# Token tiles 2 to 15 of the normalised input, transposed by DMA instead of by TensorE and ScalarE

## The chip, the core and the metric

The kernel runs on one core of one Trainium2 chip. A core has a matrix engine (TensorE, "PE" in the profile), a vector engine (VectorE, "DVE"), an activation engine (ScalarE, "ACT"), a general engine (GpSimd, "POOL") and a queue engine that starts DMA transfers (SyncE, "SP"). Each runs its own list of instructions in order, and they wait for each other by semaphores. The metric is the device time of one execution in microseconds.

## The reference, cut to what matters

One sequence of 2048 tokens with 1024 features goes through a layer norm. Its result `xn` feeds two branches: attention with 32 heads of 32 features, and a second layer norm with an MLP of 3584 hidden features. All is bf16 in and out.

```python
x = A_x                                  # 2048 x 1024
xn = _layernorm(x)
qkv = xn @ wqkv                          # q, k, v: 32 heads of 32
p = softmax(q @ k.T * 32 ** -0.5)
s = (p @ v) @ wo
y = _layernorm(xn)
h = gelu(y @ w1 + b1)                    # 3584 hidden
g = silu(h @ w2 + b2)
return x + s * g
```

Every product contracts over features, and TensorE contracts over partitions. So `xn`, which is computed with tokens on the partitions, is needed with features on the partitions. That is the transpose this case is about.

## The kernel before, in words

**An order made ahead of time.** The kernel is written as a list of operations, each with what it reads and writes, a guessed duration and a priority. The class `_Plan` runs them through a small model of the engines when the program is built (`run`), and so fixes the order of each engine's instructions. `settle` then works out the fewest semaphore waits, and `emit` (line 524 is where an instruction is put out) writes the program. The guessed durations and priorities decide the order. They do not decide when an instruction runs on the chip: there, an engine takes the next instruction of its list, waits for its semaphores and runs it. A queue is as strict for SP: a DMA that waits holds up all DMAs behind it.

**Tiles and pairs.** The 2048 tokens are 16 tiles of 128 (`NT`), and 8 pairs of tiles (`NPR`).

**The prologue** works on tiles in order:

- `load_x` (line 719): SP loads a tile of `x`, 128 x 1024 bf16, into `xst`. The tiles lie in memory that later holds the hidden activations `hT` (tiles 0 to 9) and the second-layer weights `w2r` (tiles 10 to 15), so the profile shows them under these names.
- DVE takes mean and variance: two `bn_stats` (line 860) and a `bn_aggr` (line 862) a tile, then two small operations per pair (lines 875 and 877).
- POOL takes the power -1/2 for a pair (line 879), a product (line 881), and normalises each tile (line 889) into one of four buffers `xnb[t % 4]`. Three of them lie in `gw` and the fourth in `yT`, and so the profile names them. Tiles 0 and 1 are normalised by DVE (line 870).
- `tr_item`: TensorE transposes the eight 128 x 128 blocks of a tile with an identity matrix into PSUM (line 840), and ACT copies them to `xnT`, "big" in the profile (line 851). For half of tile 1 the copy is DVE's (line 849).
- `k_pair_item`: TensorE makes the keys of head group 0 for a pair of tiles (8 matmuls, `ps<-big,qk`), and DVE casts them (line 805). `v_item` does the same for the values of a pair (16 matmuls, `ps<-qk,big`, cast in line 777), two pairs behind (`VLAG`).
- At the end of the prologue POOL computes the factors of the second layer norm for all tiles (lines 899 to 903). The last of these is a power over 128 x 16 numbers. DVE makes two diagonal matrices from it (line 944), with which `make_y` scales `xnT` for the MLP.

**Attention** runs in units. A unit is four heads, 256 queries and 256 keys. For a unit TensorE makes scores (line 1116), ACT two exponentials of 128 x 1024 (line 1125). VectorE adds up the weights of several units (lines 1146, 1151, 1154), and TensorE multiplies the weights by the values and by ones (line 700). Units run in order. The first eight, 0 to 7, use the keys of pairs 0 to 7 with the queries of pair 0, so that unit k can start once the keys of pair k are there. Between the units TensorE does the MLP products, the projections of the next heads and, at the end, the output products (line 705), spread by the planner.

**SP** also loads the weights: `load_qk` (line 730), `load_v` (line 735), `load_w1` (line 927) and `load_w2` (line 933), with priority 3.

Of the kernel before, what the change touches and what calls it, by code (L numbers as in the profile page):

```python
# [39 lines left out]
DN = ()  # L40
EVD = ()
PART = 5
ENGS = ("PE", "ACT", "DVE", "POOL", "SP")


# [18 lines left out]
class _Plan:  # L64
# [48 lines left out]
    def run(self, total_units, dense_slack):  # L113
# [7 lines left out]
        state = {"mode": "c", "bw": 0.0, "s": 0, "pv": 0, "pvopen": None, "dopen": None, "susp": None,  # L121
                 "done": 0.0, "last_bank": 7}
# [19 lines left out]
        def commit(o, t):  # L142
            e = o.eng
            o.start = t
            if e == "SP":
                if o.prio >= 5:
                    for x in reversed(order["PE"]):
                        if x.fin <= t:
                            o.deps[x] = True
                            break  # L150
                tf[e] = t + o.occ
                state["bw"] = max(state["bw"], t) + o.nbytes / 280.0
                o.fin = state["bw"] + 1900.0
            else:
                tf[e] = t + o.occ
                o.fin = t + o.occ + o.lat
            order[e].append(o)
            self.seq.append(o)
            release(o, t)
            wake(tf[e], e)  # L160
# [265 lines left out]
        while ev:  # L426
            t, ei = heapq.heappop(ev)
            e = ENGS[ei]
# [8 lines left out]
            o = pick(e, t)  # L437
# [97 lines left out]
def bass_recurrent_scan__mha_block__mixer_channel_mlp__prompt_kernel(  # L535
# [16 lines left out]
    NT = S // 128  # L552
# [12 lines left out]
    x2 = A_x.rearrange("b s d -> (b s) d")  # L565
# [6 lines left out]
    add = plan.add  # L572

    with ExitStack() as st:
# [14 lines left out]
        xnT = big[:].rearrange("p (c s) -> p c s", c=DC)  # L589
# [4 lines left out]
        wqk = [qk0[:, 4096 + i * 1024:4096 + (i + 1) * 1024].rearrange("p (c n) -> p c n", c=DC) for i in range(3)]  # L594
# [11 lines left out]
        w1r = [sb(f"w1r{i}", [128, DC, 256], BF16) for i in range(NW1R)]  # L606
# [21 lines left out]
        lnp = sb("lnp", [128, NT, 6], F32)  # L628
# [5 lines left out]
        xst = [h_flat[:, i * 1024:(i + 1) * 1024] for i in range(10)] + \  # L634
# [52 lines left out]
        def pool(fn, occ, R, W, prio=3):  # L687
            return add("POOL", fn, occ, PL, R, W, prio)

        def dma(sem, fn, nbytes, R, W, prio=3, extra=()):  # L690
            return add("SP", fn, 430, 0, R, W, prio, sem=sem, nbytes=nbytes, extra=extra)
# [18 lines left out]
        XS = lambda i: ("xst", i)  # L710
# [3 lines left out]
        for i in range(10, 16):  # L714
            lo, hi = (i - 10) * 1024, (i - 9) * 1024
            al_x[i] = [("w2", k) for k in range(NW2R) if k * 1792 < hi and (k + 1) * 1792 > lo]

        def load_x(t):
            dma(f"x{t}", lambda e: e.dma_start(xst[t], x2[t * 128:(t + 1) * 128, :]), 262144, [], [XS(t)] + al_x_w(t))

        def al_x_w(t):
            return []

        nqk = {"n": 0}

        def load_qk(hg, which):
            i = nqk["n"] % 3
            nqk["n"] += 1
            src = A_wqkv[:, which * D + hg * 128: which * D + (hg + 1) * 128].rearrange("(c p) n -> p c n", p=128)
            dma(f"wqk{i}", lambda e: e.dma_start(wqk[i], src), 262144 * 3 // 2, [], [("wqk", i)])  # L730
            return i

        def load_v(pr):
# [7 lines left out]
        for t in range(XF, 6):  # L741
            load_x(t)
        load_v(0)
        for t in range(6, NT):
            load_x(t)
        pool(lambda e: e.iota(iota_i, pattern=[[1, 128]], base=0, channel_multiplier=-1), 300, [], [("iota",)])
        dve(lambda e: e.tensor_single_scalar(ident[:], iota_i, 0, op=ALU.is_equal), 220, [("iota",)], [("ident",)], 0)
# [33 lines left out]
        def k_pair_item(n, with_q):  # L781
            return pair_item(n, (1, 0) if with_q else (1,))
# [69 lines left out]
            return it  # L852

        pro_q = plan.queues["pro"]
        XV = lambda t: ("xst", t)
        pro_q.append(warm_item())
        for n in range(NPR):
            for t in (2 * n, 2 * n + 1):
                for c in range(2):
                    dve(lambda e, t=t, c=c: e.bn_stats(stats[:, t, c, :], xst[t][:, c * 512:(c + 1) * 512]),  # L860
                        600, [XS(t)], [("st", t, c)], 1)
                dve(lambda e, t=t: e.bn_aggr(mv[:, t, :], stats[:, t, :, :].rearrange("p c s -> p (c s)")),
                    150, [("st", t, 0), ("st", t, 1)], [("mv", t)], 1)
            lo, hi = 2 * n, 2 * n + 2
            if n == 0:
                for t in (0, 1):
# [16 lines left out]
            for t in (lo, lo + 1):  # L883
                if t in DN:
                    dve(lambda e, t=t: e.tensor_scalar(xnb[t % 4], xst[t], mv[:, t, 0:1], lnp[:, t, 1:2],
                                                       op0=ALU.subtract, op1=ALU.mult), 75 + 0.26 * 1024,
                        [XS(t), ("mv", t), ("rs", n)], [("xnb", t % 4)], 0.5)
                    continue
                pool(lambda e, t=t: e.tensor_scalar(xnb[t % 4], xst[t], lnp[:, t, 1:2], lnp[:, t, 5:6],  # L889
                                                    op0=ALU.mult, op1=ALU.add), 950,  # L890
                     [XS(t), ("nb_", n), ("rs", n)], [("xnb", t % 4)], 1)
            pro_q += [tr_item(lo), tr_item(lo + 1), k_pair_item(n, False)]
            if n >= VLAG:
                pro_q.append(v_item(0, n - VLAG, "pro"))
        pro_q.append(q_pair_item(1))
# [27 lines left out]
        def load_w1(p):  # L923
            gi = p % NW1R
            pi = p % NW1
            src = B_w1[:, pi * 256:(pi + 1) * 256].rearrange("(c p) f -> p c f", p=128)
            dma(f"w1{gi}", lambda e: e.dma_start(w1r[gi][:], src), 524288, [], [("w1", gi)])

        def load_w2(q, r):
            i = nw2["n"] % NW2R  # L930
# [475 lines left out]
```

## Time and profile before

| | us |
|---|---|
| median of 3 runs | 1066.99 |
| the three runs | 1066.93 to 1067.59 |
| the profiled execution | 1066.99 |
| its span, from the first instruction to the last | 1064.9 |
| granted TensorE clock, mean | 0.996 |

The first 47 us hold the prologue. Some of the groups of the profile in that window:

| operation | line, engine | count | mean us |
|---|---|---|---|
| transposes of a block, `ps<-ident,gw` and `ps<-ident,yT` | 840, PE | 96 + 32 | 0.24 and 0.22 |
| eviction of a tile's transposes, 128 x 1024 | 851, ACT | 15 | 1.03 |
| exponential, 128 x 1024 | 1125, ACT | 15 | 1.03 |
| normalisation of a tile | 889, POOL | 14 | 1.19 to 1.41 |
| power for a pair | 879, POOL | 7 | 0.85 |

Matmuls are pipelined: eight transposes of a tile take 0.62 us together, not eight times their mean.

The DMA transfers of the first 60 us, with the median time from issue to landing: an input tile of 256 KB 4.4 us (tiles 0 to 9) and 6.7 us (tiles 10 to 15), a first-layer weight block of 512 KB 9.5 us, a second-layer weight block of 448 KB 3.7 us, the bias b2 (256 KB) 3.6 us.

How to read it: busy shares are averages over the whole span, so the share of an engine in one stage is taken from a table of windows. A timeline line gives start, length, engine, line, operation and tiles. Numbers in square brackets are the idle time of the engine before, and what ended it.

### The profile page before, as it was taken

The page shows a single profiled execution, that of the slowest core. Times are in us where ns is not written, and L with a number is a line of the kernel's source. Part 1 is how long each engine was busy: PE and PEld are TensorE (multiplying, and loading weights), DVE is VectorE, ACT ScalarE, POOL GpSimd, SP SyncE. Part 2 cuts the span into 40 slices and gives each one's busy share as a digit, 9 for nine tenths or more (in the row PEclk, how much of TensorE's full clock was granted, in tenths as well). Part 3 has the DMA queues.
Part 4 walks back from the last instruction along what each step waited for, and adds up shares of the span by engine and source line. Part 5 has one row for each costly group of instructions (what it writes and reads, how often), then busy time and mean ns, then how long its engine had stood idle before and what let it go on. Part 6 is the DMA issues. An engine that isn't in the chain of part 4 may idle for free.

```text
span 1064.9 us, 32134 instructions
## 1 busy us (share of the span) xinstructions
PE 1024.6 (96%) x14338; PEld 637.8 (60%) x14338; DVE 977.4 (92%) x1513; ACT 1024.3 (96%) x1114; POOL 34.0 (3%) x42
## 2 busy tenths in 40 slices
PE   7898999999999999999999999999999999999997
PEld 5655466646666556656666566656666566664442
DVE  8899999998899999898899999999999899978897
ACT  4899999999999999999999999999999999999993
POOL 5600000000000000000000000000000000000000
PEclk9999999999999999999999999999999999999999
DMA  9334257723276446723375446533475577772431
GB/s 267 90 105 130 59 163 202 208 82 86 79 213 184 113 113 194 200 75 105 103 201 159 142 130 188 166 90 88 134 210 166 166 236 205 220 208 89 148 110 50
DMA packets 285795, 156.48 MB, mean 147 GB/s; under 512 B 23642, under 2 KB 276570, under 8 KB 285658
## 3 DMA queue, kind: packets, MB, share of 16 engines
q1 hardware_dynamic: 285658, 154.44, 50.9%
q8 instruction: 112, 1.84, 0.7%
q14 instruction: 25, 0.20, 0.1%
HBM read 142.35 MB, written 12.06 MB: 145 GB/s over the span
## 4 chain that ended last, share of the span: by engine, by line
ACT 46%; PE 45%; DVE 4%; DMA 3%; POOL 1%; issue 0%; DVEq 0%; POOLq 0%
ACT P L1125 43%; PE ps L705 30%; PE ps L1116 8%; PE ps L700 7%; DMA w1r<-in_B_w_dram 3%; ACT ut L991 3%; DVE ut L860 1%; DVE PA L1146 0%; ACT gw L1027 0%; POOL gw L889 0%; POOL lnp L903 0%; DMA hT<-in_A_x_dram 0%; DVE xb L976 0%; DVE V L777 0%; DVE PA L1151 0%
## 5 line engine op out<-in xcount | busy, mean ns | idle before, releaser
L1125 ACT ACTIVATE P<-ps 128x1024 bf16<-128x1024 f32 x1024 | 960.9, 1198 | 10.8 <-PE ps L1116 10.5
L1146 DVE TENSOR_TENSOR PA<-P 128x2048 bf16<-128x2048 bf16 x251 | 303.9, 1212 | 17.1 <-ACT P L1125 15.9
L705 PE MATMUL ps<-yT,w1r 128*128 128x256 bf16 x1792 | 232.4, 273 | 8.7 <-DMA w1r<-in_B_w_dram 6.0
L705 PE MATMUL ps<-w2r,hT 128*128 128x256 bf16 x1792 | 228.6, 274 | 1.4 <-DVE hT L994 0.6
L705 PEld LDWEIGHTS ps<-yT,w1r 128*128 128x128 bf16 x1792 | 162.4, 98 | 67.1 <-issue 32.9
L705 PEld LDWEIGHTS ps<-w2r,hT 128*128 128x128 bf16 x1792 | 162.1, 98 | 54.6 <-issue 33.6
L700 PE MATMUL ps<-P,V 128*32 128x256 bf16 x4096 | 146.0, 275 | 0.9 <-DVE V L777 0.5
L1151 DVE TENSOR_TENSOR PA<-PA 128x1024 bf16<-128x1024 bf16 x202 | 137.9, 689 | 1.7
L705 PE MATMUL ps<-big,qk 128*128 128x512 bf16 (+2 forms) x568 | 131.2, 361 | 2.6 <-DVE V L777 0.8
L705 PE MATMUL ps<-qk,big 128*128 128x256 bf16 (+1 forms) x736 | 124.9, 306 | 0.2
L700 PEld LDWEIGHTS ps<-P,V 128*32 128x32 bf16 x4096 | 97.5, 97 | 34.8 <-issue 22.8
L1116 PE MATMUL ps<-qk 32*128 32x256 bf16 x2048 | 101.9, 273 | 8.8 <-ACT P L1125 7.0
L1116 PE MATMUL ps<-QKT 32*128 32x256 bf16 x2048 | 101.7, 273 | 4.5 <-ACT P L1125 4.3
L705 PEld LDWEIGHTS ps<-qk,big 128*128 128x128 bf16 x736 | 65.4, 98 | 39.5 <-issue 15.8
L976 DVE TENSOR_TENSOR xb<-ps,b1T 128x512 bf16<-128x512 f32 x112 | 76.8, 686 | 12.0 <-PE ps L705 10.9
L705 PEld LDWEIGHTS ps<-big,qk 128*128 128x128 bf16 x568 | 48.2, 99 | 54.3 <-issue 15.0
L994 DVE SCALAR_TENSOR_TENSOR hT<-ut,xb 128x512 bf16<-128x512 f32 x112 | 74.2, 681 | 1.9 <-ACT ut L991 1.7
L1116 PEld LDWEIGHTS ps<-QKT 32*128 32x128 bf16 x2048 | 30.3, 92 | 71.9 <-ACT P L1125 67.8
L1116 PEld LDWEIGHTS ps<-qk 32*128 32x128 bf16 x2048 | 30.4, 92 | 71.7 <-ACT P L1125 62.2
L989 DVE SCALAR_TENSOR_TENSOR ut<-hT,xb 128x1024 f32<-128x1024 bf16 x56 | 68.2, 1220 | 0.1
L991 ACT ACTIVATE ut<-ut 128x1024 f32<-128x1024 f32 x56 | 67.6, 1212 | 0.0
L1200 DVE STREAM_TRANSPOSE nt<-ps 128x256 f32<-128x256 f32 x64 | 28.7, 448 | 28.2 <-PE ps L700 27.9
(79 smaller groups left out, 574.3 us busy)
## 6 DMA issues: line engine op xcount, KB each, us to landing
w1r<-in_B_w_dram SPq DMA_DIRECT2D x112, 512.0 KB, 4.5
w2r<-in_B_w_dram SPq DMA_DIRECT2D x128, 448.0 KB, 4.3
qk<-in_A_wqkv_dram SPq DMA_DIRECT2D x16, 256.0 KB, 3.7
g_scratch<-gw SPq DMA_DIRECT2D x32, 128.0 KB, 4.5
o_scratch<-ot SPq DMA_DIRECT2D x56, 64.0 KB, 3.2
big<-o_scratch SPq DMA_DIRECT2D x28, 128.0 KB, 3.9
hT<-in_A_x_dram SPq DMA_DIRECT2D x10, 256.0 KB, 4.4
qk<-in_A_wqkv_dram SPq DMA_DIRECT2D x4, 512.0 KB, 3.9
```

Of the source, the lines that this page charges most:

```text
L700: ins = e.matmul(dst(j), lhsT=lhsT(j), rhs=rhs(j), start=start, stop=stop, tile_position=(0, 32 * j), skip_group_check=True)
L705: return e.matmul(dst, lhsT=lhsT, rhs=rhs, start=start, stop=stop, skip_group_check=True)
L860: dve(lambda e, t=t, c=c: e.bn_stats(stats[:, t, c, :], xst[t][:, c * 512:(c + 1) * 512]), 600, [XS(t)], [("st", t, c)], 1)
L976: dve(lambda e: e.tensor_tensor(xb_t[i2][:, p % 2].rearrange("p (k t) -> p k t", k=2), bank(it.bank).rearrange("p (k t) -> p k t", k=2), b ...
L989: dve(lambda e, r=r: e.scalar_tensor_tensor(ut_t[i2][:, r], h[:, r], 1.0 / GA, xb[:, r], op0=ALU.add, op1=ALU.mult), c_f32(r.stop - r.star ...
L991: act(lambda e: e.activation(ut_t[i2][:], ut_t[i2][:], ACT.Tanh, scale=GC * GA), c_acts(1024), [("ut", i2, 0), ("ut", i2, 1)], [("ut", i2, ...
L994: dve(lambda e, r=r: e.scalar_tensor_tensor(h[:, r], ut_t[i2][:, r], 1.0, xb[:, r], op0=ALU.add, op1=ALU.mult), c_f32(r.stop - r.start), [ ...
L1116: ins = e.matmul(bank(b0[j], kk * 256, (kk + 1) * 256), lhsT=QKT[sl][32 * j:32 * j + 32, 1, kb * 128:(kb + 1) * 128], rhs=QKT[sl][32 * j:3 ...
L1125: x = act(lambda e, h=h: e.activation(P[pi][:, 2 * h:2 * h + 2].rearrange("p j k q -> p (j k q)"), ps[:, pr[h] * 1024:(pr[h] + 1) * 1024], ...
L1146: add2.append(dve(lambda e, p0=p0, a0=a0: e.tensor_tensor(PA_all[:, a0:a0 + 2].rearrange("p u j q -> p (u j) q"), P_all[:, p0:p0 + 2, :, 0 ...
L1151: add4.append(dve(lambda e, a0=a0: e.tensor_tensor(PA[a0], PA[a0], PA[a0 + 1], op=ALU.add), c_b16(1024), [("PA", a0 + 1)], [("PA", a0)], P ...
L1200: a = dve(lambda e: e.transpose(nt_t[i][:], bank(pv.bank, 256, 512)), c_ps(256), [], [("nt", i)], 1, pv)
```

## The change

Tiles 0 and 1 stay with TensorE. For tiles 2 to 15 the item `tr_item` (eight transposes and an eviction) is not queued. In its place SP gets a DMA transpose that reads `xnb[t % 4]` and writes the tile's place in `xnT`, both in SBUF. It waits for the normalisation on POOL, and the key and value products wait for it. The next normalisation into the same buffer, four tiles later, waits for it as well. Its priority is 0, ahead of the loads (3), and the planner reckons with 1500 ns on SP, 360000 bytes and a latency of 2600 ns, where a load has 430 ns, its own bytes and 1900 ns.

The loads change their place. Input tiles 8 to 15 are each loaded after the first statistics of the tile eight before (`XA`, `XB`). The first three blocks of the first-layer weights wait for the normalisation of tiles 9, 11 and 13 (`XW`), and the third `load_qk` waits for that of tile 15.

In the order of the built program, SP has the loads of tiles 8 to 14, then the 14 transposes (with the load of tile 15 behind the second), and only then the weight loads. On POOL the power and product of tiles 8 and 9 come ahead of the normalisation of tiles 6 and 7, and the later powers and products are ahead by one to two tiles in the same way. Two of the three small operations for the second layer norm come ahead of the normalisation of tile 15. On DVE the casts of keys and values come later among the statistics.

```diff
+TD = 2
+XA = 8
+XB = 8
+XW = 9
...
-                o.fin = state["bw"] + 1900.0
+                o.fin = state["bw"] + (2600.0 if o.sem.startswith("tp") else 1900.0)
...
-        def load_x(t):
-            dma(f"x{t}", lambda e: e.dma_start(xst[t], x2[t * 128:(t + 1) * 128, :]), 262144, [], [XS(t)] + al_x_w(t))
-
-        def al_x_w(t):
-            return []
+        def load_x(t, R=()):
+            dma(f"x{t}", lambda e: e.dma_start(xst[t], x2[t * 128:(t + 1) * 128, :]), 262144, R, [XS(t)])
...
-            dma(f"wqk{i}", lambda e: e.dma_start(wqk[i], src), 262144 * 3 // 2, [], [("wqk", i)])
+            dma(f"wqk{i}", lambda e: e.dma_start(wqk[i], src), 262144 * 3 // 2, [], [("wqk", i)], 3,
+                [xnop[NT - 1]] if nqk["n"] == 3 else [])
...
-        for t in range(6, NT):
+        for t in range(6, XA):
             load_x(t)
...
+                for k in range(XA, NT):
+                    if max(0, k - XB) == t:
+                        load_x(k, [("st", t, 0)])
...
-                pool(lambda e, t=t: e.tensor_scalar(xnb[t % 4], xst[t], lnp[:, t, 1:2], lnp[:, t, 5:6],
+                xnop[t] = pool(lambda e, t=t: e.tensor_scalar(xnb[t % 4], xst[t], lnp[:, t, 1:2], lnp[:, t, 5:6],
...
-            pro_q += [tr_item(lo), tr_item(lo + 1), k_pair_item(n, False)]
+            for t in (lo, lo + 1):
+                if t < TD:
+                    pro_q.append(tr_item(t))
+                else:
+
+                    add("SP", lambda e, t=t: e.dma_start_transpose(out=xnT[:, :, t * 128:(t + 1) * 128], in_=xnb[t % 4]),
+                        1500, 0, [("xnb", t % 4)], [("xnT", t, h) for h in range(2)], 0, sem=f"tp{t % 4}", nbytes=360000)
+            pro_q.append(k_pair_item(n, False))
...
-            dma(f"w1{gi}", lambda e: e.dma_start(w1r[gi][:], src), 524288, [], [("w1", gi)])
+            dma(f"w1{gi}", lambda e: e.dma_start(w1r[gi][:], src), 524288, [], [("w1", gi)], 3,
+                [xnop[XW + 2 * p]] if p < 3 else [])
```

## The prediction

> **What bounds the kernel now.** I first read the busy shares and then the windows cut at the events that turned out to matter (columns: window, length, busy us of PE, PEld, DVE, ACT and POOL with instruction counts, granted clock, DMA share, GB/s).
>
> ```profile
> PE 1024.6 (96%) x14338; PEld 637.8 (60%) x14338; DVE 977.4 (92%) x1513; ACT 1024.3 (96%) x1114; POOL 34.0 (3%) x42
> ...
> 34.64:40.76 6.12, 3.77 (x48) 2.52 (x45) 5.51 (x8) 4.46 (x5) 6.04 (x7) 1.00 0.25 75
> 40.76:46.73 5.97, 5.01 (x56) 3.67 (x57) 3.81 (x8) 3.90 (x5) 3.84 (x3) 1.00 0.67 182
> 46.73:1047.64 1000.91, 976.37 (x13881) 605.76 (x13879) 925.21 (x1395) 994.62 (x1082) 0.00 (x0) 1.00 0.52 146
> 1047.64:1064.90 17.26, 10.51 (x62) 4.64 (x61) 12.24 (x22) 0.01 (x1) 2.27 (x2) 0.93 0.17 61
> ```
>
> PE and ACT look equally full on average, but the windows separate the stages. From 46.73 to 1047.64 us ACT works 994.62 of 1000.91 us: it is the bound there, with 6.3 us of gaps in all. The last 17.3 us have no exponential left. So the span is (when ACT becomes dense) + 1000.9 + 17.3, and an edit to the first 47 us counts only by how it moves that first moment. ACT becomes dense with attention unit 7: units run in order, unit k needs the keys of token pair k, and in both programs 14 exponentials (units 0 to 6) stand before unit 7 on ACT. The 14 evictions that go (15.1 us for the 15 whole ones in the first 47 us, L851) lie in a stage where ACT is waiting, so their time isn't itself a gain.
>
> Next, what brings tile 15 and then unit 7, from the timeline of POOL, DVE, PE and ACT (start, length, engine, line, operation):
>
> ```profile
> 20.54 0.70 POOL L879 TENSOR_TENSOR lnp<-lnp,mhalf 128x2 f32<-128x2 f32 x1
> 21.31 0.19 POOL L881 TENSOR_TENSOR lnp<-lnp 128x2 f32<-128x2 f32 x1
> 21.61 1.19 POOL L889 TENSOR_SCALAR gw<-hT,lnp 128x1024 bf16<-128x1024 bf16 x1
> 22.79 1.19 POOL L889 TENSOR_SCALAR yT<-hT,lnp 128x1024 bf16<-128x1024 bf16 x1
> 24.11 0.70 POOL L879 TENSOR_TENSOR lnp<-lnp,mhalf 128x2 f32<-128x2 f32 x1
> ...
> 34.64 1.73 POOL L879 TENSOR_TENSOR lnp<-lnp,mhalf 128x2 f32<-128x2 f32 x1
> 36.45 0.88 POOL L881 TENSOR_TENSOR lnp<-lnp 128x2 f32<-128x2 f32 x1
> 37.29 0.69 POOL L899 TENSOR_TENSOR lnp<-mv,lnp 128x16 f32<-128x16 f32 x1
> 37.96 1.19 POOL L889 TENSOR_SCALAR gw<-w2r,lnp 128x1024 bf16<-128x1024 bf16 x1
> 39.14 1.62 POOL L889 TENSOR_SCALAR yT<-w2r,lnp 128x1024 bf16<-128x1024 bf16 x1
> ```
> ```profile
> 23.88 0.15 DVE L875 TENSOR_SCALAR lnp<-mv 128x2 f32<-128x2 f32 x1
> ...
> 34.60 1.21 DVE L1146 TENSOR_TENSOR PA<-P 128x2048 bf16<-128x2048 bf16 x1
> ```
> ```profile
> 44.81 0.48 DVE L944 TENSOR_SCALAR qk<-identf,lnp 128x128 f32<-128x128 f32 x2 [1.11 <-POOL lnp L903]
> 45.21 0.68 DVE L1151 TENSOR_TENSOR PA<-PA 128x1024 bf16<-128x1024 bf16 x1
> 45.81 0.42 DVE L805 CAST qk<-ps 128x256 bf16<-128x256 f32 x1
> 46.28 0.12 PEld L1116 LDWEIGHTS ps<-qk 32*128 32x128 bf16 x8 [0.87 <-DVE qk L805]
> 46.28 0.40 PE L1116 MATMUL ps<-qk 32*128 32x256 bf16 x8 [0.59 <-DVE qk L805]
> ...
> 46.73 1.02 ACT L1125 ACTIVATE P<-ps 128x1024 bf16<-128x1024 f32 x1 [1.29 <-PE ps L1116]
> ```
>
> **POOL sets the pace of the start.** Per token pair it does a power (0.78 us to the next start), a product (0.30) and two normalisations (1.18 each): 3.57 us from 20.54 to 24.11, without a pause from 13.42 to 40.76 us. DVE keeps to that pace because its small fast operations can't run while POOL holds a normalisation (L875 at 19.39 takes 1.06 us instead of 0.15 and ends with POOL's tile 5), and the reverse: when DVE starts its additions (L1146, 34.60), POOL's power takes 1.73 us instead of 0.70. From 34.64 the five POOL operations need 0.78 + 0.30 + 0.25 + 2.37 = 3.7 us by their undisturbed rows, and took 6.12: 2.4 us lost to that. Tile 15 is normalised at 40.76, unit 7 starts 5.97 us later.
>
> **The change, part by part.** All rows are of one execution, span 1064.9 us; the median of the runs is 1066.99, 2.1 us more, and I add shifts of the span to the median.
>
> *PE and ACT lose 14 tile transposes*: 14 x 8 matmuls (0.62 us a tile) and 14 x 1.02 us of ACT. Neither sets the pace in those 47 us: at 39.21 PE's own wait is for POOL. Worth 0 by itself. If POOL were not in the way, ACT's 14 us would show.
>
> *POOL's work is the same, its order isn't.* In the changed program the power and product of tiles 8 and 9 stand before the normalisation of tiles 6 and 7, and POOL takes its instructions in order. That power needs DVE's statistics of tile 9, at 23.88 us before. DVE reaches them earlier now, because a key cast (0.34) and a value cast (0.59) went behind: 22.95. The power can start at 23.2, POOL having been free from 21.6; with 1.07 for power and product, tile 6 starts at 24.25 instead of 21.61. Of the 2.64 us, 1.07 are work done early; 1.57 are lost. From there POOL's rows give: tiles 6, 7 to 26.62; power and product of 10, 11, then tiles 8, 9 to 30.2; power of pair 6, tile 10, product, tile 11 to 33.85.
>
> *The tail of POOL.* Left then: pair 7's power and product, tiles 12 to 15, and three operations on the second norm's factors (L899, L901, L902), two of which stood behind tile 15 before. Work: 0.78 + 0.30 + 4 x 1.19 + 0.25 + 0.32 + 0.30 = 6.7, from 33.95 to 40.65 without DVE. DVE's order again puts two 2048-wide and two 1024-wide additions there: 2 x 1.21 + 2 x 0.68 = 3.8 us of holding at most, 0 at least; I take the 2.4 us that the same four cost before: tile 15 normalised at 43.05 (40.65 to 44.5).
>
> *From tile 15 to unit 7.* DVE's order now is: the diagonals (L944), which need POOL's last power (2.95 us, L903), then key cast of pair 6, value cast, a 2048-wide addition, key cast of pair 7. From 43.05: power ends 46.1, diagonals 46.55, cast 46.9, value cast 47.5, addition 48.65. On PE, behind the scores of unit 6 (47.0), stand 4 value matmuls, the 8 of key pair 7 (0.87), 8 value matmuls (0.87), then unit 7. These fill the time to 49.5; the key cast at 48.7 to 49.1 is hidden in it. Scores and start of ACT add 0.5: unit 7 at 50.0, against 46.73: **+3.3 us** (T = 40.65 gives 47.5, +0.8; T = 44.5 gives +4.8).
>
> *Units 1 to 5* come later too: the key cast of pair 1 now stands behind the statistics of tile 13 on DVE, about 27.8 us (20.4 before), and PE's value products are queued behind unit 1's scores. ACT has 22 us from there for 12 exponentials of 1.02 us, so none of that reaches unit 7. The transpose of b1 (L938) moves up to PE's start; its input is issued as early: 0.
>
> *The transposes themselves* are seen in no row. Each is a 256 KB move inside SBUF, issued by SP, which waits for POOL in order. Below: the plain 256 KB loads, 0.43 us of SP and 3.6 us to land (b2b, alone). Above: the first-layer weights, 9.5 us to land and 5.90 / 3 = 1.97 us of SP each. A normalisation waits until the transpose four tiles before has landed. POOL's own pace leaves 4 x 1.78 - 1.3 = 5.8 us for that, and 1.96 us of SP per tile (tile 6 at 25.43 to tile 15 at 43.05). With the 4.4 us of the input loads, to which I hold (same size, same queue, half the bytes of the slow row), everything is hidden, even for tile 15: 43.05 + 0.2 + 4.4 = 47.65, when PE gets there. Cost 0. With 9.5 us, buffer 3 goes: tile 3 issued 17.9, landed 27.4; tile 7 landed 38.2; tile 11 landed 48.9; tile 15 normalised 50.1, landed 59.7; unit 7 at 61.7: +15.
>
> *SP's queue.* The weight loads go behind all transposes, to about 44 us instead of 13.3 to 19.3. Their first user, the first MLP product, was at 60.15 us; 9.5 us to land still leaves 6. Input tiles 8 to 15 go out one by one behind DVE's statistics of eight tiles before; tile 12's goes out at about 12 us and is needed at 25. Cost 0; without that cover a late weight load would cost its lateness once.
>
> *After unit 7*, 18 value matmuls are left for PE instead of 33, 15 x 0.11 = 1.65 us less, beside an ACT that is full: 0. Sum: 1066.99 + 3.3 = **1070.3 us**.
>
> **Rivals.** *The transposes set the pace* (20%): for it, 14 of them on one in-order queue, and no row shows one; against, the DMA share is 0.25 to 0.44 from 20.5 to 40.8 us, so there is room. From 5.8 us of landing on it decides; at 9.5 us +15, 1082; in the middle, 7.7 us, 1074 to 1077. The Trainium skill (VectorE: DVE Perf Modes, "The three transpose paths") gives 1309 ns for one 128x128 block by DMA and 390 ns by TensorE; eight in a row would be an estimate of 10.5 us a tile and about 120 us more in all, while the page Advanced Engine Details and Errata ("X-Bar Transpose (TRN2)") calls such DMAs as fast as plain ones, which leaves my sum as it stands. No run here shows either yet.
>
> *POOL ends undisturbed* (16%): the additions of DVE fall into POOL's waits and tile 15 is done at 40.65, unit 7 at 47.5: 1067.8, no change. For it, the scores that feed these additions come later than before; against, the four additions still stand ahead of the last power in DVE's order.
>
> *Faster: ACT's gaps close* (12%). The place is 46.73 to 1047.64, the price at most its 6.3 us of idle ACT, all of it waiting for scores from PE. PE enters with 1.65 us less to do and with a newly planned order. It takes over half of the gaps (3.3 us) before the loss at the start is covered; all of them give 1064.0. Against: the gaps lie spread over 900 us, far from the work removed.
>
> **How the numbers follow.** Forecast 52%: 1067.9 to 1071.8 by its own bounds, widened to 1074 since a new order moves gaps by a few us. A measurement can tell about 0.2%, 2.1 us. Faster: most of the third rival, 0.12. Same: the second, and a sixth of the forecast's weight (little contention): 0.24. Slower: 0.64. The range leaves out the best of the faster cases and transposes near the upper bound: 1065.5 to 1081.
>
> **What would show it.** Right: POOL idle for about 1.6 us before the power of pair 4; tile 6 near 24.3; tile 15 normalised near 43; the first exponential of unit 7 near 50; ACT dense from there for about 1001 us. Wrong: POOL waiting for transposes (landing above 5.8 us, or SP over 1.96 us each), unit 7 before 47, or a gap sum on ACT that differs from 6.3 us by more than 3.

## The result and the profile after

| | before | changed |
|---|---|---|
| median of the runs, us | 1066.96 (4 runs, 1065.52 to 1067.59) | 1072.01 (4 runs, 1070.72 to 1073.35) |
| ratio, 95% interval | | 1.0049 (1.0032 to 1.0067) |
| the profiled execution, its span, us | 1066.99, 1064.9 | 1072.81, 1071.0 |

The change costs 0.3 to 0.5 per cent, a small loss that is clear of the noise in two measurements. A second measurement on another chip, 12 runs beside 29 of the kernel before, gave 1.0032 (1.0018 to 1.0046); its profiled execution has a span of 1069.4 us and is called "the second execution" below.

The changed kernel's windows, cut at the same events as before (window, length, busy us of PE, PEld, DVE, ACT and POOL with instruction counts, granted clock, DMA share, GB/s):

```profile
20.98:35.05 14.07, 10.29 (x69) 6.89 (x67) 12.36 (x34) 2.58 (x3) 10.57 (x15) 0.67 0.80 143
35.05:44.32 9.27, 8.43 (x89) 6.25 (x87) 8.59 (x11) 5.93 (x7) 9.18 (x9) 1.00 0.72 91
44.32:51.67 7.35, 5.31 (x56) 4.00 (x57) 4.14 (x8) 3.12 (x4) 3.38 (x2) 1.00 0.82 180
51.67:1052.82 1001.15, 975.58 (x13810) 603.11 (x13808) 928.06 (x1402) 994.71 (x1082) 0.00 (x0) 1.00 0.53 149
1052.82:1071.00 18.18, 11.38 (x66) 4.95 (x64) 13.64 (x24) 0.00 (x1) 2.28 (x2) 0.91 0.16 58
```

ACT has lost its 14 evictions (1011.3 us busy over the span, 1024.3 before), but the stage that ACT bounds is as long as it was: 1001.15 us with 994.71 of work. It starts at 51.67 in place of 46.73. Since the first exponential of unit 0 moves by half a microsecond from one execution to the next, the useful figure is the interval from it to unit 7's. The loss then adds up, in two executions of the changed kernel against the one of before:

| us | before | changed | second execution |
|---|---|---|---|
| first exponential of unit 0 | 13.77 | 14.22 (+0.45) | 13.34 (-0.43) |
| from there to unit 7 | 32.96 | 37.45 (+4.49) | 36.50 (+3.54) |
| unit 7 to the last exponential's end | 1000.91 | 1001.15 (+0.24) | 1001.44 (+0.53) |
| from there to the end of the span | 17.30 | 18.16 (+0.86) | 18.15 (+0.85) |
| span | 1064.9 | 1071.0 (+6.1) | 1069.4 (+4.5) |

The last row of the windows ends at a rounded span; the table has the instruction's own end. Two executions of one kernel differ by 0.95 us in the second row, so smaller differences between single profiles say little; the part on PE's clock shows where the 0.95 us comes from. Most of the loss is in the prologue; 0.9 us is at the very end.

The prologue first. POOL's timeline in the changed kernel (start, length, engine, line, operation; in brackets the idle time before it and what ended it; line 884 is the power, 894 the normalisation, 915 the last power):

```profile
23.62 0.70 POOL L884 TENSOR_TENSOR lnp<-lnp,mhalf 128x2 f32<-128x2 f32 x1 [1.67 <-DVE lnp L882]
24.56 1.19 POOL L894 TENSOR_SCALAR gw<-hT,lnp 128x1024 bf16<-128x1024 bf16 x1
...
35.05 0.70 POOL L884 TENSOR_TENSOR lnp<-lnp,mhalf 128x2 f32<-128x2 f32 x1 [1.23 <-DVE lnp L882]
35.73 2.27 POOL L894 TENSOR_SCALAR gw<-w2r,lnp 128x1024 bf16<-128x1024 bf16 x1
...
43.16 1.19 POOL L894 TENSOR_SCALAR yT<-w2r,lnp 128x1024 bf16<-128x1024 bf16 x1
44.32 3.38 POOL L915 TENSOR_TENSOR lnp<-lnp,mhalf 128x16 f32<-128x16 f32 x1
```

POOL, which had no pause before, now has two: it waits 1.67 us for pair 4's statistics while tiles 6 and 7 stand behind that power, and 1.23 us for pair 7's. Tile 12 takes 2.27 us, with DVE's 2048-wide addition beside it; undisturbed tiles take 1.19. Tile 15 is done at 44.32, 3.56 us later than before.

Behind tile 15, the timelines of DVE (957 diagonals, 807 key cast) and ACT (1138 exponential; its line 1129 is PE's scores):

```profile
47.73 0.48 DVE L957 TENSOR_SCALAR qk<-identf,lnp 128x128 f32<-128x128 f32 x2 [2.84 <-POOL lnp L915]
48.13 0.42 DVE L807 CAST qk<-ps 128x256 bf16<-128x256 f32 x1
```
```profile
49.05 1.94 ACT L1138 ACTIVATE P<-ps 128x1024 bf16<-128x1024 f32 x2 [3.55 <-PE ps L1129]
51.67 22.18 ACT L1138 ACTIVATE P<-ps 128x1024 bf16<-128x1024 f32 x24 [0.68 <-PE ps L1129]
```

DVE stands idle for 2.84 us in front of two diagonal matrices that only the MLP needs, and the key casts of pairs 6 and 7 are queued behind them. ACT waits 3.55 us for unit 6. Behind unit 6's scores PE has 20 products of keys and values, and then come unit 7's scores; pair 7's key cast (50.46 to 50.88 us) is hidden in that time.

The transposes themselves, in the changed kernel's list of DMA issues (count, median us from issue to landing):

```profile
big<-gw SPq DMA_TRANSPOSE x10, 3.1
big<-yT SPq DMA_TRANSPOSE x4, 3.2
```

They take 1.23 to 1.46 us of SP each (two of them 1.83 and 2.56, the median is 1.27) and land 2.7 to 5.2 us after issue. POOL waits for none. PE waits for them twice, 3.84 us for the first ones and 1.08 us for pair 6's, and neither wait reaches unit 7: after the first PE stands idle again in any case, for 3.78 us, and behind the second DVE casts pair 6's keys only after POOL's last power. The DMA engines have less room than before: their mean busy share from 20.98 to 35.05 us is 0.80, and 0.40 in the same 14 us of the kernel before.

The end of the span. PE's last unbroken stretch of output products behind the last attention products, in the kernel before and in the changed one:

```profile
1048.26 3.63 PE L705 MATMUL ps<-qk,big 128*128 128x512 bf16 x16
```
```profile
1053.67 4.27 PE L709 MATMUL ps<-qk,big 128*128 128x512 bf16 x19
```

The newly planned order leaves three more of these for the end, 0.64 us of PE; the stretch starts 0.61 us after the last exponential before, and 0.85 us after it now. Together that is the 0.9 us of the table's fourth row. It returned in every profile: 18.15 or 18.16 us in the eleven of the changed kernel and its variants, 17.25 to 17.30 us in the three of the kernel before and its variants. No run put the three products back, so that this order is the cause is read from the profiles and not shown by an experiment.

### The profile page after: what moved, and what is told of

The parts are those of the page before. It is cut to its first block, busy times and chain, and to the rows that moved or that the text cites. A ratio compares the mean times of both kernels' runs of the same rounds, so it can differ in the third digit from the quotient of the medians.

```text
span 1071.0 us, 31821 instructions
## 1 busy us (share of the span) xinstructions
PE 1024.5 (96%) x14174; PEld 633.6 (59%) x14174; DVE 983.4 (92%) x1523; ACT 1011.3 (94%) x1100; POOL 34.2 (3%) x42
## 4 chain that ended last, share of the span: by engine, by line
ACT 78%; PE 17%; DVE 3%; DMA 1%; POOL 1%; issue 0%; DVEq 0%
ACT P L1138 72%; PE ps L709 11%; ACT ut L1004 4%; PE ps L1129 3%; PE ps L704 3%; DVE ut L862 1%; DMA w1r<-in_B_w_dram 1%; ACT gw L1040 1%; POOL gw L894 0%; POOL lnp L915 0%; DMA hT<-in_A_x_dram 0%; DVE lnp L880 0%; DVE w1r L1279 0%; DVE mv L864 0%; DVE xb L989 0%
## 5 line engine op out<-in xcount | busy, mean ns | idle before, releaser
L1159 DVE TENSOR_TENSOR PA<-P 128x2048 bf16<-128x2048 bf16 x254 | 307.6, 1213 | 21.1 <-ACT P L1138 19.3
L1164 DVE TENSOR_TENSOR PA<-PA 128x1024 bf16<-128x1024 bf16 x209 | 143.0, 691 | 1.2
L709 PE MATMUL ps<-big,qk 128*128 128x512 bf16 (+2 forms) x568 | 134.4, 369 | 2.7 <-DMA big<-gw 1.1
L709 PE MATMUL ps<-qk,big 128*128 128x256 bf16 (+1 forms) x736 | 128.2, 313 | 5.1 <-DMA big<-gw 3.8
L709 PEld LDWEIGHTS ps<-qk,big 128*128 128x128 bf16 x736 | 67.4, 100 | 47.2 <-issue 17.3
L709 PEld LDWEIGHTS ps<-big,qk 128*128 128x128 bf16 x568 | 50.7, 102 | 54.6 <-issue 15.2
```

The lines of the kernel that those rows point to most:

```text
L709: return e.matmul(dst, lhsT=lhsT, rhs=rhs, start=start, stop=stop, skip_group_check=True)
L1159: add2.append(dve(lambda e, p0=p0, a0=a0: e.tensor_tensor(PA_all[:, a0:a0 + 2].rearrange("p u j q -> p (u j) q"), P_all[:, p0:p0 + 2, :, 0 ...
L1164: add4.append(dve(lambda e, a0=a0: e.tensor_tensor(PA[a0], PA[a0], PA[a0 + 1], op=ALU.add), c_b16(1024), [("PA", a0 + 1)], [("PA", a0)], P ...
```

## The experiments

Three theories: A, the new order of POOL's and DVE's lists sets unit 7; B, the DMA transposes set the pace; C, the new order behind unit 7 costs the time. In the first runs the finished lists are edited: `move(o, a)` takes an operation out of its engine's list and puts it right behind another, so that nothing else changes. The lines of the variants are shifted by a few: 810 is the key cast, 897 (901 in the variants with ACT) the normalisation, 918 POOL's last power, 960 the diagonals, 1133 the scores and 1142 the exponential. In e4, a variant of the kernel before, 882 is the power, 808 the key cast and 843 the transposes. Each was timed against the kernel before on the same chip.

| kernel | ratio to before, 95% interval | unit 0 to unit 7, us |
|---|---|---|
| before | 1 | 32.96 |
| changed, first and second measurement | 1.0049 (1.0032 to 1.0067), 1.0032 (1.0018 to 1.0046) | 37.45, 36.50 |
| e1: POOL's list in the old order | 1.0027 (1.0014 to 1.0039) | 35.22 |
| e2: diagonals behind pair 7's key cast | 1.0023 (1.0012 to 1.0033) | 35.71 |
| e3: PE's first gap filled | 1.0039 (1.0024 to 1.0054) | 36.55 |
| h4: both of PE's gaps filled | 1.0035 (1.0022 to 1.0048) | 35.81 |
| e4: POOL's hold alone, in the kernel before | 1.0045 (1.0031 to 1.0060) | 38.51 |
| e1, e2 and e3 together | 1.0004 (0.9991 to 1.0017) | 34.29 |
| the same, second gap filled too | 1.0004 (0.9990 to 1.0017) | 33.67 |
| the same three, pair 1's key cast early | 1.0016 (1.0004 to 1.0027) | 34.68 |
| f1a: odd tiles normalised by ACT | 0.9969 (0.9956 to 0.9981) | 32.29 |
| f1b: f1a with values cast by ACT | 0.9976 (0.9965 to 0.9987) | 32.42 |
| g1: odd tiles by ACT, transposes by TensorE | 1.0023 (1.0010 to 1.0037) | 36.88 |

**POOL's order (e1).** The changed kernel, with each power and product back behind the tiles of the pair before, and the small operations of the second norm behind tile 15 (one of the three stood ahead of tile 14 in the kernel before).

```diff
+        for n in range(2, NPR):
+            move(pw[n], xnop[2 * n - 1])
+            move(mu[n], pw[n])
+        move(s2[0], xnop[NT - 1])
+        move(s2[1], s2[0])
+        move(s2[2], s2[1])
```

> The changed kernel, with POOL's list put back into the order of before (power and product of a pair, then its two normalisations; the operations for the second norm behind tile 15). All other lists stay. Theory A (the order on POOL and DVE sets unit 7): no wait ahead of the power of pair 4 while tile 6 is ready; tile 15 normalised at about 41.6 us instead of 44.3, unit 7 at about 49.2 instead of 51.7, so about 2.5 us less than the changed kernel, ratio to before about 1.0025. Theory B (the DMA transposes set the pace): normalisations now wait for landings, tile 15 stays near 44 and the time stays at a ratio of 1.005. Theory C (the newly planned order behind unit 7 costs the time): unit 7 may move, the ratio stays at 1.005.

Measured: 35.22 us from unit 0 to unit 7, 1.3 to 2.2 below the changed kernel's two executions, and a ratio of 1.0027. Tile 15 is done at 39.85, 4.5 us earlier than in the first execution (4.1 counted from unit 0), more than I had expected. Unit 7 gains only half of that. The three small operations, now behind tile 15, take 2.28 us, so the last power starts at 42.13 and not at 44.32, and DVE still stops in front of the diagonals, which need that power. Its timeline in e1:

```profile
45.12 0.48 DVE L960 TENSOR_SCALAR qk<-identf,lnp 128x128 f32<-128x128 f32 x2 [1.67 <-POOL lnp L918]
```

**The diagonals (e2).** The changed kernel with the two diagonals behind pair 7's key cast on DVE.

```diff
+        move(dgo[0], kc[1, NPR - 1])
+        move(dgo[1], dgo[0])
```

> The changed kernel, with only the two diagonals (which need POOL's last power) moved on DVE from ahead of the key cast of pair 6 to behind that of pair 7. Theory A: the cast of pair 6 runs at about 46 us instead of 48.1, unit 6 at 46.3, unit 7 at about 49.9 instead of 51.7, 1.8 us less, ratio about 1.0032. Theory B: pair 6 and 7 wait for their transposes anyway, unit 7 stays within 0.5 us of 51.7. Theory C: ratio stays at 1.005 although unit 7 moves.

Measured: 35.71 us, 0.8 to 1.7 less, ratio 1.0023. POOL's waits of 1.67 and 1.23 us are still there, as in the first execution, so the difference to that one, 1.7 us, is the like-for-like price. The diagonals come right behind the last key cast, and a transpose takes the place of the wait for them. DVE's timeline, then PE's:

```profile
47.83 0.48 DVE L960 TENSOR_SCALAR qk<-identf,lnp 128x128 f32<-128x128 f32 x2
```
```profile
43.34 1.05 PE L709 MATMUL ps<-big,qk 128*128 128x256 bf16 x8 [0.79 <-DMA big<-gw]
```

PE's key products of pair 6 wait 0.79 us for tile 13's transpose, which takes 4.69 us to land here, and from there PE has no pause of note until unit 7's scores. So with the diagonals out of the way the landing of one transpose is on the path.

**PE's clock (e3, h4).** I had not foreseen that PE would stand idle until the first transposes land (3.84 us, to 19.98) and again in front of unit 1's scores (3.78 us, to 28.06), nor that the granted clock would then be lower: it is 0.67 on average from 20.98 to 35.05 us, and 1.00 before the change. Eight key products took 1.86 us in place of 1.05. I put about 1 us of the loss down to this at first. In e3 the first gap is filled with products of the identity, and in h4 both are.

```diff
+        scrap(vit[0, 1], vit[0, 1].chunks[0], 17)
```

(`scrap` puts so many products into an item's bank, ahead of the operation named; in h4 a second call puts 17 ahead of unit 1's scores.)

> The changed kernel, with 17 more matmuls of the identity (512 columns, nothing reads them) on PE between the values of pair 0 and those of pair 1, where PE waits 3.8 us for the first transposes and its granted clock then falls to 0.5. If the fallen clock is part of the loss: the granted clock between 20 and 24 us is 1.0 instead of 0.5 to 0.67, the key cast of pair 2 no longer waits for PE, POOL's wait before the power of pair 7 (1.23 us) shrinks to under 0.4, unit 7 comes about 1 us earlier, ratio about 1.004. If it is not (DVE's list holds everything up anyway): the clock rises, unit 7 stays within 0.3 us of 51.7.

> The changed kernel with products of the identity (read by nothing) in both of PE's gaps, and its lists otherwise unchanged. A2 (the clock is one of three losses, and POOL's order and the diagonals are the others): the clock stays near 1.00 from 20 to 34 us, and unit 0 to unit 7 falls little below the 36.55 us of the run with the first gap filled, to 35.8 to 36.5 us, since POOL's wait for pair 7's statistics was down to 0.26 us there; ratio 1.0025 to 1.0040. If the clock were the whole loss: 33 us and 1.000.

> The changed kernel once more, beside the two others, on one chip. Every theory: a ratio of 1.0032 to 1.0067, the interval of the first measurement, and unit 0 to unit 7 within 0.6 us of 37.45 us.

The repeat kept to its ratio but missed its interval: 36.50 us is 0.95 below the first execution, and 0.6 were allowed. Windows of 2 us (columns as above), in the first execution of the changed kernel, in its second, and in h4, which ran beside the second on the same chip:

```profile
28.00:30.00 2.00, 1.94 (x15) 1.16 (x16) 2.00 (x6) 1.27 (x2) 2.00 (x3) 0.50 0.70 132
...
32.00:34.00 2.00, 2.00 (x15) 1.34 (x17) 1.07 (x3) 0.00 (x0) 1.82 (x3) 0.61 0.62 139
```
```profile
28.00:30.00 2.00, 2.00 (x14) 1.47 (x12) 2.00 (x8) 1.57 (x2) 1.74 (x3) 0.57 0.70 141
...
32.00:34.00 2.00, 2.00 (x25) 1.51 (x24) 1.51 (x6) 1.43 (x2) 1.73 (x3) 1.00 0.58 131
```
```profile
28.00:30.00 2.00, 2.00 (x21) 1.78 (x20) 2.00 (x8) 1.62 (x2) 1.74 (x3) 1.00 0.68 137
```

With PE kept busy (h4) the clock is 1.00 throughout, so the idle time did lower it. In the other two it falls at the second gap, but not for as long: it is back at 1.00 at about 33.6 us in the first execution and 31.7 us in the second. What that does is seen in DVE's timelines in the first and the second execution, and then POOL's in the second:

```profile
32.45 0.42 DVE L807 CAST qk<-ps 128x256 bf16<-128x256 f32 x1 [1.19 <-PE ps L709]
```
```profile
30.64 0.42 DVE L807 CAST qk<-ps 128x256 bf16<-128x256 f32 x1 [0.25 <-PE ps L709]
```
```profile
33.21 0.70 POOL L884 TENSOR_TENSOR lnp<-lnp,mhalf 128x2 f32<-128x2 f32 x1 [0.27 <-DVE lnp L882]
```

PE starts unit 1's scores 13.84 us after unit 0's first exponential in both executions, so what differs is how long it then runs slowly. The cast stands ahead of pair 7's statistics on DVE. While PE is slow DVE waits for PE's products, and POOL then waits for the statistics: 1.23 us in the first execution and in e2, where the clock is low for about 6.8 us (worked out from such windows), 0.27 and 0.26 us in the second execution and in e3, where it is low for about 3.4 us, and not at all in h4. The difference of 0.96 us is the 0.95 us between the two executions of one kernel. So e3's 36.55 us is no gain against the second execution (36.50): filling the first gap alone shows none. In the interval to unit 7 the clock costs 0.7 to 1.6 us, h4's 35.81 us against the two executions. The measured times neither show nor exclude this: 1.0035 for h4 beside 1.0032, with intervals of 0.0013 and 0.0014 to each side.

**POOL's hold alone (e4).** The kernel before, with nothing changed but tiles 6 and 7 behind pair 4's power and product on POOL.

```diff
+        move(xnop[6], mu[4])
+        move(xnop[7], xnop[6])
```

> The kernel before, with TensorE's transposes, and on POOL only the normalisation of tiles 6 and 7 moved behind the power and product of pair 4, as in the changed kernel. Theory A: POOL waits about 1.6 us for DVE before that power, tile 15 and unit 7 come about 1.6 us later than before (unit 7 at about 48.3 instead of 46.7), the time rises by about 1.6 us, ratio about 1.0015. Theories B and C: no transpose by DMA and no new plan is in it, so the ratio is 1.000 within 0.0005.

This missed by far: 5.55 us, where 1.6 were expected. The timelines of POOL, PE and DVE in e4:

```profile
23.32 0.70 POOL L882 TENSOR_TENSOR lnp<-lnp,mhalf 128x2 f32<-128x2 f32 x1 [2.60 <-DVE lnp L880]
```
```profile
25.53 1.03 PE L843 MATMUL ps<-ident,gw 128*128 128x128 bf16 x8 [3.04 <-POOL gw L892]
```
```profile
28.30 0.42 DVE L808 CAST qk<-ps 128x256 bf16<-128x256 f32 x1 [4.32 <-PE ps L705]
```

The old list of PE has the transposes of tile 6 ahead of pair 2's key products, and the old list of DVE has the cast of those keys ahead of the statistics of the next pair. So holding tile 6 stops PE for 3.04 us and DVE for 4.32 us, and that stops POOL again, for 3.37 us. Part of it is PE's clock, which is 0.50 from 26 to 30 us here; how much was not separated. So this run does not price the hold in the changed kernel, where DVE's casts stand further back. It shows that such a hold is paid again at each list that was made for another order.

**All three together.** The changed kernel with the edits of e1, e2 and e3.

> The changed kernel with all three edits of the first set together: POOL's list in the order of the kernel before, the two diagonals behind pair 7's key cast, and 17 products of the identity on PE ahead of pair 1's values (read by nothing). A (the order of POOL's and DVE's lists and PE's clock set unit 7; the DMA transposes themselves cost nothing): the single gains were 2.23, 1.74 and 0.90 us of the 37.45 us from unit 0's first exp to unit 7's, so 31.5 to 33.5 us, against 32.96 in the kernel before; ratio to before 0.9985 to 1.0010. B (the transposes by DMA set the pace): at most the largest single gain, 35 us or more, ratio 1.002 or above. If the edits all act on the same last link and do not add, 34 to 35 us and 1.001 to 1.002.

Measured: 1.0004, the time of the kernel before, with all 14 transposes still done by DMA. Theory B falls, since 34.29 us is below its 35, and C is left with the 0.9 us at the end. But the gains do not add: 34.29 us, in the range that the expectation gave for that case. And the equal time is in part luck: against the kernel before, the profiled execution loses 1.3 us from unit 0 to unit 7 and 0.9 us at the end, and wins 2.9 us by shorter waits of ACT behind unit 7 (3.0 us in place of 6.3), at which no edit was aimed. What binds now, in two windows of this kernel, to unit 1's first exponential and from there to unit 7's:

```profile
13.66:29.26 15.60, 9.29 (x66) 5.39 (x65) 15.60 (x38) 1.94 (x3) 14.25 (x19) 0.98 1.06 225
29.26:47.95 18.69, 18.69 (x185) 14.07 (x185) 15.26 (x32) 11.63 (x13) 14.52 (x14) 0.93 0.69 141
```

In the first window PE does 9.29 us in 15.60, of which 3.84 are the added products; in the second it is busy all the time. PE has taken POOL's place: 4.23 us of its early idle time is a wait for pair 1's key cast, which DVE has behind the statistics of later tiles.

Two runs on top of it asked whether that gap is the rest of the loss: once with PE's second gap filled (for the clock), once with the key cast moved up by seven statistics operations.

> The kernel with all three edits, and 17 more products of the identity (read by nothing) on PE ahead of unit 1's scores, where PE stood idle for 4.23 us. In the run with all three edits the granted clock was 0.62 and 0.52 from 28 to 32 us, and PE was busy without a break from 29 us to unit 7. A2 (what is left of the loss is PE's clock after that second gap): 3.4 us of PE time at about 0.57 hold 1.9 us of work at full clock, so 1.5 us come back: unit 0 to unit 7 about 32.8 us in place of 34.29 (32.96 in the kernel before), ratio 0.9985 to 0.9998. C2 (PE would be late at full clock too, or the list of DVE holds it): 34 to 34.5 us and 1.0000 to 1.0010. If the granted clock still falls with PE kept busy, the idle time was not what lowered it.

> The kernel with all three edits, and the key cast of pair 1 on DVE taken ahead of seven statistics operations, to about 23.9 us in place of 28.14. There PE waited 4.23 us for that cast, in order, with the products of later pairs behind it, and was busy without a break from 29 us to unit 7. A3 (once POOL's and DVE's lists are mended, PE's work of the prologue is the bound, and the late cast of pair 1 is what makes PE late): PE starts on it 4 us earlier, then POOL's tiles bound it again; unit 0 to unit 7 32.3 to 33.3 us in place of 34.29, ratio 0.9985 to 1.0000. C3 (PE would end there anyway, or POOL's list is still the bound): 34 to 34.6 us and a ratio of 1.0000 to 1.0010. The ratios of both lie within the measurement's uncertainty of each other; the interval from unit 0 to unit 7 and PE's waits tell them apart.

Filled, the clock stays at 1.00, and unit 7 comes after 33.67 us, between the two expectations; the ratio stays 1.0004. With the cast moved up, PE's wait does not go but moves on by one pair, to 4.44 us in front of unit 2, and the products behind it are slow (16 in 3.15 us; undisturbed, 1.9). 34.68 us and 1.0016: no gain. One cast is not enough, and I did not try to move them all; whether PE would then end earlier stays open.

**Relieving POOL (f1a, f1b, g1).** If POOL's 14 normalisations set the pace, then ACT, which the change has freed, should take some. In f1a the odd tiles are normalised by ACT. The order is planned anew with 1190 ns for a normalisation on POOL, each power held behind the even tile of the pair before, the diagonals late, the first weights of both MLP layers behind tiles 14 and 15, and the 17 products of e3.

```diff
+                if t % 2:
+                    xnop[t] = act(lambda e, t=t: e.activation(xnb[t % 4], xst[t], ACT.Identity, scale=lnp[:, t, 1:2], bias=lnp[:, t, 5:6]),
...
+                    continue
```

> The changed kernel, its order planned anew, with the odd tiles normalised by ACT (scale and bias from lnp) in place of POOL, POOL's powers held behind the even tile of the pair before, the diagonals behind pair 7's key cast, the first output weights behind tiles 14 and 15, and the 17 products of the identity. A (POOL's 16 normalisations in a row set the pace before unit 7, and ACT has room since the change): POOL loses 8 x 1.19 = 9.5 us, ACT gains 8 x about 1.2 us in place of the 14 evictions taken from it; DVE's casts and statistics become the limit, so unit 0 to unit 7 some 31.5 us (32.96 before) and a ratio of about 0.9985. B (the transposes set the pace): as in the run with all three edits, no gain over it.

(The expectation counts 16 normalisations and 8 odd tiles; POOL has 14, and ACT takes 7 of them, at 1.24 us each.)

0.9969 (0.9956 to 0.9981): faster than both kernels, by little. Unit 7 comes after 32.29 us, little better than before (31.5 expected). Of the 4.9 us by which the profiled span is shorter (1060.0 us), 0.7 come from there and 1.0 from an earlier first unit; 4.1 come from fewer waits of ACT behind unit 7 (996.82 us with 994.34 of work), and 0.9 are lost at the end. The waits behind unit 7 vary among all these kernels, 2.5 to 6.7 us; why f1a has few was not tested. POOL and ACT now do wait for transposes to free their buffers, 2.8 and 4.0 us in all, so at this pace the landing time is no longer hidden.

f1b also takes the value casts of pairs 1 to 5 from DVE to ACT.

> The kernel with odd tiles on ACT, and the value casts of pairs 1 to 5 on ACT as well. A (once POOL is relieved DVE's work before unit 7 is the limit): DVE loses 5 casts of about 0.7 us, 3 to 3.5 us; unit 0 to unit 7 28.6 to 29.5 us and a ratio of about 0.9965. B (the transposes set the pace): the same time as the kernel with odd tiles on ACT, within 0.0015.

It gains nothing (0.9976, 32.42 us). DVE was not the limit there: from 30.16 us to unit 7 PE works 15.17 of 15.26 us. Theory B expected equal times too, and at this pace it is not excluded: POOL waits 2.1 us and ACT 4.1 us for transposes to free their buffers here.

g1 is the control: the kernel before, TensorE and ACT transposing, with f1a's normalisation, its order of POOL and its late diagonals, but without the late weights and the added products.

> The kernel before (tiles 2 to 15 transposed by TensorE, evicted by ACT) with the odd tiles normalised by ACT and the same order of POOL and DVE. If the gain of the kernels with odd tiles on ACT comes from POOL's relief alone, this one gains as much: unit 0 to unit 7 31.5 us, ratio 0.9985. If it needs the room that the DMA transposes made on ACT: 14 evictions of 1.19 us, 7 or 8 normalisations of 1.2 us and the exps of units 0 to 6 fill ACT, unit 0 to unit 7 34 to 37 us, ratio 1.001 to 1.004.

1.0023, slower than before. The windows from unit 0 to unit 7, of f1a and then of g1:

```profile
12.77:45.06 32.29, 26.65 (x252) 18.91 (x250) 29.07 (x69) 21.68 (x22) 19.91 (x25) 1.00 0.89 192
```
```profile
12.98:49.86 36.88, 33.83 (x370) 25.69 (x369) 30.38 (x72) 34.02 (x35) 19.22 (x25) 1.00 0.62 176
```

POOL is relieved alike in both (19.91 and 19.22 us, 29.07 before). In g1 ACT is busy 34.02 of 36.88 us with evictions, normalisations and exponentials; in f1a 21.68. So the room that the DMA transposes make on ACT has a use, and the change as it stands leaves it idle. How much of the 4.6 us between the two intervals it is worth was not separated from the late weights, the added products and the other plan of f1a.

## Why the prediction was right, point by point

The forecast was 1070.3 us, slower by 3.3; measured were 1072.0, and by the second ratio 1070.4. The mechanism was the predicted one, with two terms missing: the end of the program and PE's clock. With both left out, that 1070.4 comes so near is in part luck.

- **Only the shift of unit 7 counts, because ACT is dense behind it.** Right: the dense stage grew by 0.2 to 0.5 us. The constant 17.3 us behind it was not constant, however. The last stretch grew by 0.9 us in every kernel that was planned with the change. I had let a newly planned order move the waits by "a few us" in the range, but had not looked at how it ends, though the lists would have told that three output products were moved there. This is one missing term.
- **POOL's hold of 1.57 us.** Right: 1.67 us in both executions, power at 23.62 (23.2 predicted), tile 6 at 24.56 (24.25). e1, which takes the hold and the order behind it away, shows that POOL's list costs 2.2 us against the first execution, in which PE's clock was low for as long as in e1, and 1.3 against the second.
- **POOL's tail and the 2.4 us lost to DVE's additions.** Right: from pair 7's power to tile 15's end 9.27 us, 6.7 without disturbance, so 2.57 lost. Tile 15 ended at 44.32 (43.05 predicted) in the first execution, in which unit 0 was late by 0.45 and POOL waited 1.23 us for pair 7's statistics, and at 42.49 in the second, with a wait of 0.27. The prediction had no such wait. It comes from PE's clock and is the other missing term.
- **Tile 15 to unit 7.** The path was right: last power, diagonals, pair 6's key cast, then PE's products behind unit 6, with pair 7's key cast hidden in them. Predicted 6.95 us from tile 15 to unit 7 at 50.0; measured 7.35 in both executions, to 51.67 and 49.84. The power took 3.38 us, not the 2.95 of the row that I used. e2 shows that the diagonals cost 1.7 us, 0.8 against the second execution, since the casts need not wait for them.
- **The transposes, cost 0.** Right for the changed kernel, where no wait for them reaches unit 7. Bounds 0.43 to 1.97 us of SP: the median is 1.27, with one of 2.56 above the bound. I held to 4.4 us of landing, between 3.6 and 9.5; the median is 3.2, below the lower bound, and the longest, 5.2, lies near the 5.8 from which they would decide. The plain 256 KB loads were the right row to be nearest to. Two things show that the margin is thin: the wait of 0.79 us in e2, and the waits for buffers in f1a.
- **The first rival, transposes as the pace:** refuted for the changed kernel by POOL's timeline and by the run with all three edits. The argument against it was weaker than it looked, since the DMA engines, 0.25 to 0.44 busy before, are 0.80 busy from 20.98 to 35.05 us. It is also what the Trainium skill's figure would have given (VectorE: DVE Perf Modes, "The three transpose paths": 1309 ns for a block of 128 x 128). Eight blocks together take 1.27 us of SP and 3.2 us to land here, so its figure does not multiply by the blocks of a tile.
- **The second rival, POOL undisturbed:** refuted, 2.57 us were lost. **The third, ACT's gaps close:** refuted for the changed kernel, 6.44 us after 6.3. They do close in part in other variants with the same work behind unit 7 (3.0 us with all three edits), for a reason that stays open.
- **Units 1 to 5 late, worth nothing.** Right as far as ACT goes, which was the reason given. But PE, late and at a low clock, holds up DVE ahead of pair 7's statistics, and through them POOL: 1.23 and 0.27 us. Once POOL's and DVE's lists are mended, the late key casts leave PE idle early, and PE is the next bound.
- **SP's queue.** Right: the first MLP product came at 61.54 (60.15 before) and waited for its input from DVE, not for weights.

## What to carry to other kernels

Work that is taken off an engine with slack buys nothing by itself; look for the engine that sets the pace of the stage (here POOL, 29 of 33 us) and use the freed engine for its work. When a planner makes the order anew, compare every engine's list with the old one, the end of the program too: a power ahead of two tiles and two diagonals ahead of two casts cost more here than the operations that were moved take. When work leaves an engine, look where it now pauses, and whether another engine's list waits for what it does next. After an edit that removes one wait, look for the engine that is full next, and expect single gains not to add.

## What the runs showed of the hardware

- **PE's granted clock falls after a pause of 2 to 4 us, for about 3.4 or about 6.8 us.** In the changed kernel PE stops at 24.3 us for 3.78 us; the clock is 1.00 from 24.3 to 26.7 and 0.50 from 26.8 to 33.5 us. After a pause of 2.26 us in the second execution it is 0.57 from 28 to 32 us, and in e4, with a pause of 3.04 us, 0.50 from 26 to 30 us. With the pauses filled it stays at 1.00 (h4). The Trainium skill has such a rule (TensorE: Matmul & The Clock Gate, "Part 1: The HAM clock gate": half rate after an idle window of about 3.4 us). The traces agree with it in kind, but here the clock also fell after pauses of 2.26 and 3.04 us, and 2.5 us into that of 3.78 us. It cost 0.7 to 1.6 us of the interval to unit 7, although PE was not the bound of that stage, because DVE's list and then POOL's waited for what PE made.
- **A DMA transpose of a 128 x 1024 bf16 tile inside SBUF** lands in 3.2 us (2.7 to 5.2) and takes SP 1.27 us (1.23 to 2.56). The input tiles of 256 KB, loaded from memory in the first 20 us of the same execution, land in 4.6 to 4.8 us, and 256 KB loads of weights over the whole execution in 2.9 to 3.1.
- **DVE's additions and POOL's operations hold each other up.** POOL's normalisation took 2.27 us beside a 2048-wide addition of 1.22 us and 1.19 us alone. In the other direction, small operations of DVE that take 0.15 us alone took up to 1.06 us beside a normalisation.
